# Outputs of two plain f-tiles at a time, a bank each, and weights made in thirds through PSUM

## The chip, the cores and the metric

The kernel runs on one core of a Trainium2 chip. TensorE (PE) multiplies, VectorE (DVE), ScalarE (ACT) and GpSimd (POOL) do elementwise work, and SyncE (SP) issues nearly all DMAs. PE reads its stationary and its moving operand from SBUF and writes to PSUM, which has 8 banks here, one tile of 128x512 floats in each. The metric is the device time of one execution in microseconds: the median of three runs before is 549.28 (547.87 to 549.73). The profiled execution took 550.31, of which 548.5 are the span from the first to the last instruction; 1.8 lie around it.

## The reference

Three stages follow each other. Decayed attention over blocks of 64 positions (2 x 8 heads, 768 positions, width 64):

```python
intra = einsum('bhij,bhjd->bhid', einsum('bhic,bhjc->bhij', qb, kb) * Dmask, vb)
inter = einsum('bhid,bhde->bhie', qb * lam_pow, kv_state)
out[:, :, sl] = intra + inter
kv_state = lam_block * kv_state + einsum('bhsd,bhse->bhde', kb * rev_pow, vb)
```

Its output, as x of 1536 tokens x 512, goes through a gated layer and then a maximum of three:

```python
xn = x / sqrt(mean(x * x) + 1e-6) * rms_g
x = (silu(xn @ w_gate) * (xn @ w_val)) @ w_out      # d_ff 1536: 12 f-tiles of 128
out = max(x @ w1, x @ w2, x @ w3) @ w_out2          # d_ff 768
```

## The kernel before

Every matrix product is made of three (`mm3`): each operand is split into a high part (`wh`, `xh`, `hh`) and the rest (`wl`, `xl`, `hl`), and high by high, high by low and low by high are summed in PSUM. Tokens go in 3 blocks of 512 columns.

**Attention** goes in 12 chunks of 128 tokens. One chunk passes through ten pieces, named by letters: T transposes q and k, C makes scores and state updates, a, b and V mask them and advance the state, M makes the output, U and N norm it, R subtracts to get `xl`, K scales keys. `orders` says in which order the pieces of neighbouring chunks are issued. Chunks 0 to 4 and parts of 5 and 6 run ahead of the gated layer (the loop at L972, here the opening); the rest are issued between the products of blocks 0 and 1, by `gap()`, which is called after every sixth product.

**Weights.** Each tile of weights (a unit: `g` gate, `v` value, `o` output) is loaded as raw 64-bit words (`wraw`, three buffers), made into floats (ACT L238 and L239, DVE L196, L199 and L202, POOL L204), then split: ACT casts `wh` (L167), POOL subtracts to get `wl` (L170). Before, the first stage makes them with `make_unit`, one whole unit at every second `gap()` of block 0, and with `narrow` set the intermediate `mid` lies in SBUF, in W's own place; in the opening it lies in PSUM.

**First stage.** The first four f-tiles are plain: for each block, each f-tile makes `pg` and `pv` (12 products each), gates them, and its 12 output products are added to four accumulators (`acc`) that stay in four banks until the block's four f-tiles are through. Outputs of an f-tile are issued after the next one's `pg` and `pv`. Later f-tiles, and the maxout, use 7 products of half tiles in place of 8; that second stage is not touched but for the very last output tile (`out2`).

Engines take their instructions in the order in which the program issues them, so the order of issue is the order of each queue. The banks are given to tiles as they come free.

Of the kernel before, what the change touches and what calls it, by code (L numbers as in the profile page):

```python
# [18 lines left out]
P = 128  # L19
# [7 lines left out]
def tile_decay_attention_swiglu_maxout(  # L27
# [89 lines left out]

    groups1 = [4]
    PLAIN = sum(groups1)
    unit_list = [(nm, f) for f in range(PLAIN) for nm in "gvo"]  # L120
    for f in range(PLAIN, F1):
        unit_list += [("g", f), ("v", f), ("o", f - 1) if f > PLAIN else None, ("Tg", f), ("Tv", f)]
    unit_list += [("1", 0), ("1", 1), ("o", F1 - 1), ("T1", 0), ("T1", 1), ("2", 0), None, ("2", 1), ("3", 0), ("T2", 0),
# [23 lines left out]
    mid = {}  # L147
    sums_in = {}
    room = [WBUFS, 8]
    pos = {"load": 0, "made": 0, "raw": 0, "step": 0, "gap": 0, "quiet": False, "lag": 3, "narrow": True, "seam": False}  # L150

    def load_to(n):
        while pos["load"] < min(n, len(raw_list)):
# [62 lines left out]
    def begin_unit():  # L216
# [4 lines left out]
        if first_use[key] <= pos["step"] + 6 and at < len(wpools) and (key is None or room[at]):  # L221
# [20 lines left out]
    def make_unit():  # L242

        if stage2:
            finish_unit(*stage2.pop(0))
        if stage1:
            unit = stage1.pop(0)
            for n in range(3):
                words_of_unit(n, *unit)
            stage2.append(unit[:3])  # L250
        begin_unit()

    thirds = []

# [165 lines left out]
    def rest(c):  # L420
# [7 lines left out]
    named = dict(M=(2, mixed), N=(3, normed), C=(1, scores), a=(1, masked(0)), R=(3, rest),  # L428
                 b=(1, masked(1)), U=(2, summed), V=(1, advance), T=(0, lambda c: (loads_to(c + 2), turn(c))),
                 K=(-1, decayed_keys))  # L430
    orders = ["MCaNbTURVK"] * (CPNB + 2) + ["MCaNRbTUVK"] + ["MNCRaUbVTK"] * NCH
    attn_q = [(s_, named[ch][1], s_ - named[ch][0]) for s_ in range(NCH + 3) for ch in orders[s_]
              if (ch == "K") <= s_ - named[ch][0] < NCH]
    gaps = [0, 0]
# [7 lines left out]
    def gap():  # L442


        pos["gap"] += 1
        if not pos["quiet"]:
            if lates:
                third_of_unit()
            elif (pos["gap"] + 5) % (2 if pos["step"] < groups1[0] else 4) == 0:
                make_unit()  # L450
        due.sort(key=lambda e: e[0])
        while due and due[0][0] <= pos["gap"]:
            due.pop(0)[1]()
# [18 lines left out]
    def proj(ps, unit, bh, bl):  # L472
        wh, wl = unit
        for kk in range(KD):
            ks = slice(kk * P, (kk + 1) * P)
            mm3(ps, wh[:, ks], wl[:, ks], bh[:, kk, :], bl[:, kk, :], kk == 0, kk == KD - 1)
            if kk % 2:
                gap()

    def split(dst_h, dst_l, src):  # L480
        nc.scalar.copy(out=dst_h, in_=src)  # L481
# [10 lines left out]
    def drain1(acc, g, j):  # L492
        if g == 0:
            acc_sb[j] = act.tile([P, KD, NB], F32, tag="acc", name="acc_sb", bufs=3)
        for m in range(KD):
            if g == 0:
                nc.scalar.copy(out=acc_sb[j][:, m, :], in_=acc[m])
            else:
                nc.vector.tensor_tensor(out=acc_sb[j][:, m, :], in0=acc[m], in1=acc_sb[j][:, m, :], op=ALU.add)

    def stage_end(j, acc):

# [102 lines left out]
    def hidden1(f, j):  # L605
        bh, bl = x_block(j)
        pg = bank("pg")
        proj(pg, units["g", f], bh, bl)
        pv = bank("pv")
        proj(pv, units["v", f], bh, bl)  # L610
        if j == NBLK - 1:
            free(("g", f), ("v", f))
        sg = act.tile([P, NB], F32, tag="sg", name="sg", bufs=1)
        nc.scalar.activation(out=sg, in_=pg, func=AF.Silu)
        nc.vector.tensor_tensor(out=sg, in0=pv, in1=sg, op=ALU.mult)  # L615
        return sg

    def out1(acc, f, f0, f1, hh, hl):
        wh, wl = units["o", f]
        for m in range(KD):  # L620
            ms_ = slice(m * P, (m + 1) * P)
            mm3(acc[m], wh[:, ms_], wl[:, ms_], hh, hl, f == f0, f == f1)
            if m % 2:
                gap()

    def first_stage():

        acc = []
        before = None
        for now in steps:  # L630
            if now:
                pos["step"] = steps.index(now)
                g, j, f, f0, f1 = now
                if g == 0 and f == f0:
                    while attn_q and attn_q[0][0] <= 6 + 4 * j:
                        attn_step()
                    if j < NBLK - 1:
                        gaps[:] = [(6 * groups1[0], 16)[j], 6 + 4 * (j + 1)]
                if pos["step"] == len(steps) - 1:
                    pos["narrow"] = True  # L640
                r = hidden1(f, j)
                hh = act.tile([P, NB], F32R, tag="hh", name="hh")
                hl = act.tile([P, NB], F32R, tag="hl", name="hl")
                split(hh, hl, r)
                if before:
                    finish()

                def finish(now=now, hh=hh, hl=hl):
                    g, j, f, f0, f1 = now
                    if f == f0:  # L650
                        acc[:] = [bank("acc") for _ in range(4)]
                    out1(acc, f, f0, f1, hh, hl)
                    if f == f1:
                        drain1(acc, g, j)
                    if j == NBLK - 1:
                        free(("o", f))
            before = now
        return finish

# [187 lines left out]
    def out2(g, j, t):  # L847
        last = g == F2 // 2 - 1
        if g == 0 and t == 0:
            acc_sb[j] = act.tile([P, KD, NB], F32, tag="acc", name="acc_sb", bufs=3)  # L850
        ts = slice(t * P, (t + 1) * P)
        acc = bank("acc")
        for d in range(2):
# [4 lines left out]
            nc.tensor.matmul(out=acc, lhsT=hh[:, ts], rhs=wh, start=d == 0, stop=False)  # L858
            nc.tensor.matmul(out=acc, lhsT=hh[:, ts], rhs=wl, start=False, stop=False)  # L859
            nc.tensor.matmul(out=acc, lhsT=hl[:, ts], rhs=wh, start=False, stop=d == 1)  # L860
        y = acc_sb[j][:, t, :]
        if g == 0:
            nc.scalar.copy(out=y, in_=acc)
        else:
            nc.vector.tensor_tensor(out=y, in0=acc, in1=y, op=ALU.add)
        if last:
            r0 = j * NB + t * P
            nc.sync.dma_start(out=out[r0:r0 + P, :], in_=y)
# [75 lines left out]
    with tc.manual_schedule():  # L944
# [27 lines left out]
        for s_ in range(CPNB + 3):  # L972
            if stage1:
                unit_ = stage1.pop(0)
            while attn_q[0][0] == s_:
                fn = attn_q[0][1]
                attn_step()
                if unit_ and fn is named["b"][1]:
                    words_of_unit(0, *unit_)
                elif unit_ and fn is named["U"][1]:  # L980
                    words_of_unit(1, *unit_)
                    if stage2:
                        finish_unit(*stage2.pop(0))
# [6 lines left out]
        pos["narrow"] = True  # L990
        finish = first_stage()
        pos["step"] = len(steps)
        second_stage(finish)
# [31 lines left out]
```

## Time and profile before

| | us |
|---|---|
| median of 3 runs | 549.28 |
| profiled execution | 550.31 |
| its span | 548.5 |
| PE busy | 529.8 (97%) |
| DVE busy | 376.5 (69%) |
| POOL busy | 316.3 (58%) |
| ACT busy | 278.6 (51%) |

A busy PE is pipelined: a product of 512 columns is listed with 0.39 us, but one follows another after 0.23. The shares are means over stages with other limits: the opening ends and the first stage starts at 42.5 us in this execution, attention's last piece on PE is at 128.4. In the profile's rows, "x32" of a 64x64 product stands for 16 products, each in two passes.

### The profile page before, as it was taken

To read this page: it belongs to the slowest core of one execution; us is meant where nothing else is said; L and a number is where in the kernel's file an instruction comes from. 1 tells how busy PE (TensorE), PEld (TensorE's weight loads), DVE (VectorE), ACT (ScalarE), POOL (GpSimd) and SP (SyncE) were. 2 spreads that over 40 slices of the span, in tenths; PEclk is the share of its full clock that TensorE was granted. 3 is DMA by queue.
4 is the path that set the end of the run, shared out by engine and by line. 5 is a ranking of instruction groups with operands and counts; after the bars stand their busy time and mean duration, and the time that the engine had idled before them with its cause. 6 is when DMAs were issued, how large, how long until landed. Compare 5 with 4: busy or idle time off the path is not lost.

```text
span 548.5 us, 9716 instructions
## 1 busy us (share of the span) xinstructions
PE 529.8 (97%) x3722; PEld 438.9 (80%) x3722; DVE 376.5 (69%) x663; ACT 278.6 (51%) x541; POOL 316.3 (58%) x251
## 2 busy tenths in 40 slices
PE   7697979999999999999999999999999999999997
PEld 7685858878888888888888888888888888888885
DVE  6688995447795666657776686877777477684464
ACT  3576754344556665255446426556466755651120
POOL 2469996212899557165455736986387554962050
PEclk9978999999999999999999999999999999999999
DMA  8987566000212222121221312121123222300014
GB/s 193 231 195 185 140 179 155 2 3 0 78 34 82 78 67 86 39 76 39 78 76 39 115 39 77 40 76 38 40 78 114 82 76 75 83 33 0 0 55 176
DMA packets 65454, 44.67 MB, mean 81 GB/s; under 512 B 40064, under 2 KB 61568, under 8 KB 65408
## 3 DMA queue, kind: packets, MB, share of 16 engines
q1 hardware_dynamic: 64704, 44.05, 28.3%
q8 instruction: 29, 0.48, 0.4%
q14 instruction: 17, 0.14, 0.1%
q10 hardware_dynamic: 704, 0.01, 0.1%
HBM read 40.90 MB, written 3.15 MB: 80 GB/s over the span
## 4 chain that ended last, share of the span: by engine, by line
PE 85%; POOL 4%; issue 3%; DVE 3%; SPq 2%; ACT 2%; DMA 1%; POOLq 0%; ACTq 0%
PE p L676 34%; PE r L676 8%; PE acc L468 6%; PE acc L470 6%; PE acc L469 6%; PE q L676 4%; PE acc L859 3%; PE acc L858 3%; PE acc L860 3%; PE pv L468 2%; PE pv L469 2%; PE pv L470 2%; PE pg L468 2%; SPq L92 2%; PE pg L470 2%
## 5 line engine op out<-in xcount | busy, mean ns | idle before, releaser
L170 POOL TENSOR_TENSOR wl<-W,wh 128x512 fp32r<-128x512 f32 x77 | 105.6, 1371 | 39.4 <-ACT wh L167 39.2
L204 POOL TENSOR_TENSOR W<-W,wraw 128x512 int32<-128x512 int32 x60 | 81.3, 1356 | 79.3 <-DVE W L202 70.8
L167 ACT CAST wh<-W 128x512 fp32r<-128x512 f32 x77 | 47.8, 621 | 85.3 <-POOL W L204 84.9
L482 POOL TENSOR_TENSOR hl<-sg,hh 128x512 fp32r<-128x512 f32 x36 | 48.5, 1348 | 25.7 <-ACT hh L481 25.7
L676 PE MATMUL p<-xh,wh 128*128 128x512 f32 x148 | 57.6, 389 | 0.0
L676 PE MATMUL p<-xl,wh 128*128 128x512 f32 x148 | 57.6, 389 | 0.0
L676 PE MATMUL p<-xh,wl 128*128 128x512 f32 x148 | 57.6, 389 | 0.0
L468 PE MATMUL acc<-hh,wh 128*128 128x512 f32 x144 | 56.5, 393 | 0.0
L469 PE MATMUL acc<-hl,wh 128*128 128x512 f32 x144 | 56.1, 389 | 0.0
L470 PE MATMUL acc<-hh,wl 128*128 128x512 f32 x144 | 56.1, 389 | 0.0
L831 DVE TENSOR_TENSOR acc_sb<-acc,acc_sb 128x512 f32<-128x512 f32 x46 | 31.8, 691 | 21.6 <-PE acc L470 20.6
L238 ACT ACTIVATE W<-wraw 128x512 f32<-128x512 f32 x60 | 40.2, 670 | 6.8 <-DMA wraw<-in_moe_w_dram 4.3
L481 ACT CAST hh<-sg 128x512 fp32r<-128x512 f32 x36 | 22.3, 620 | 35.0 <-DVE sg L615 26.4
L239 ACT ACTIVATE wraw<-wraw 128x512 int32<-128x512 uint32 x60 | 39.7, 662 | 0.0
L731 ACT COPY c<-p 128x512 f32<-128x512 f32 x34 | 20.0, 588 | 38.1 <-PE p L676 38.0
L482 POOL TENSOR_TENSOR hl<-m,hh 128x512 fp32r<-128x512 f32 x18 | 24.0, 1343 | 23.0 <-ACT hh L481 22.9
L196 DVE TENSOR_SCALAR mid<-W 128x512 f32<-128x512 f32 x50 | 34.2, 685 | 3.0 <-ACT W L238 3.0
L199 DVE TENSOR_SCALAR mid<-mid 128x512 int32<-128x512 int32 x50 | 34.7, 694 | 0.7
L676 PE MATMUL p<-yh,wh 128*128 128x512 f32 x90 | 35.0, 389 | 0.0
L676 PE MATMUL p<-yl,wh 128*128 128x512 f32 x90 | 35.0, 389 | 0.0
L676 PE MATMUL p<-yh,wl 128*128 128x512 f32 x90 | 35.0, 389 | 0.0
L202 DVE SCALAR_TENSOR_TENSOR W<-wraw,mid 128x512 int32<-128x512 int32 x50 | 34.0, 680 | 1.0
(175 smaller groups left out, 1349.1 us busy)
## 6 DMA issues: line engine op xcount, KB each, us to landing
wraw<-in_moe_w_out_dram SPq DMA_DIRECT2D x18, 512.0 KB, 3.4
wraw<-in_moe_w_dram SPq DMA_DIRECT2D x18, 512.0 KB, 3.6
kn<-in_k_dram SPq DMA_DIRECT2D x12, 256.0 KB, 4.3
qn<-in_q_dram SPq DMA_DIRECT2D x12, 256.0 KB, 5.3
vn<-in_v_dram SPq DMA_DIRECT2D x12, 256.0 KB, 4.2
wraw<-in_moe_w_gate_dram SPq DMA_DIRECT2D x12, 256.0 KB, 3.0
wraw<-in_moe_w_gate_dram SPq DMA_DIRECT2D x24, 128.0 KB, 3.6
wraw<-in_moe_w_val_dram SPq DMA_DIRECT2D x12, 256.0 KB, 3.0
```

Source lines behind the costliest of these rows:

```text
L167: nc.scalar.copy(out=wh, in_=W.bitcast(F32))
L170: nc.gpsimd.tensor_tensor(out=wl, in0=W.bitcast(F32), in1=wh.bitcast(F32), op=ALU.subtract)
L196: nc.vector.tensor_scalar(out=mid[key].bitcast(F32), in0=W.bitcast(F32), scalar1=LEAST, scalar2=MOST, op0=ALU.max, op1=ALU.min)
L199: nc.vector.tensor_scalar(out=mid[key], in0=mid[key], scalar1=0x07FFFFFF, scalar2=3, op0=ALU.bitwise_and, op1=ALU.logical_shift_left)
L204: nc.gpsimd.tensor_tensor(out=W, in0=W, in1=lo, op=ALU.add)
L238: nc.scalar.activation(out=W.bitcast(F32), in_=hi.bitcast(F32), func=AF.Abs)
L239: nc.scalar.activation(out=lo, in_=lo.bitcast(U32), func=AF.Copy, scale=2.0 ** -29)
L468: nc.tensor.matmul(out=out, lhsT=wh, rhs=xh_, start=first, stop=False)
L469: nc.tensor.matmul(out=out, lhsT=wh, rhs=xl_, start=False, stop=False)
L470: nc.tensor.matmul(out=out, lhsT=wl, rhs=xh_, start=False, stop=last)
L482: nc.gpsimd.tensor_tensor(out=dst_l, in0=src, in1=dst_h.bitcast(F32), op=ALU.subtract)
L676: nc.tensor.matmul(out=ps, lhsT=w[:, ks], rhs=r[:, o + k, :], start=first and k == 0 and n == 0, stop=k == 1 and n == 2, skip_group_check= ...
```

## The change

Blocks 0 and 1 hold two f-tiles' `hh` and `hl` and then make their outputs together (`out_two`): for each of four output slices one bank takes both f-tiles' six products, and is then copied to SBUF (first pair, ACT) or added to it (second pair, DVE). This is issued between the next f-tile's `pg` and `pv`. Block 2 stays as it was. The list of units follows: two `g` and `v`, then two `o`, and one `g` ahead of the `o`. `spread()` is called after every third product; it issues attention's pieces, and a third of a unit in three calls of four. `narrow` stays off until the last step, so that `mid` lies in PSUM. In the opening, weights are loaded and begun one chunk later. In step 0 the products with `xl` come last. The last output tile of the kernel is made and stored in two halves of 256 columns. Not shown here: the lines of `hidden1` that only move code into it.

```diff
-    unit_list = [(nm, f) for f in range(PLAIN) for nm in "gvo"]
+    unit_list = []
+    for f in range(0, PLAIN, 2):
+        unit_list += [("g", f), ("v", f), ("g", f + 1), ("v", f + 1), ("o", f), ("o", f + 1)]
+        if f:
+            unit_list.insert(6 * f // 2 - 2, unit_list.pop(6 * f // 2))
...
-    orders = ["MCaNbTURVK"] * (CPNB + 2) + ["MCaNRbTUVK"] + ["MNCRaUbVTK"] * NCH
+    orders = ["MCaNbTURVK"] * (CPNB + 2) + ["MCNRabTUVK"] + ["MNCRaUbVTK"] * NCH
...
             if lates:
                 third_of_unit()
-            elif (pos["gap"] + 5) % (2 if pos["step"] < groups1[0] else 4) == 0:
-                make_unit()
         due.sort(key=lambda e: e[0])
         while due and due[0][0] <= pos["gap"]:
             due.pop(0)[1]()
+        spread()
+
+    def spread():
+        pos["half"] += 1
+        if not lates and pos["half"] % 4:
+            third_of_unit()
         if gaps[0]:
...
+        todo = [(kk, w, x) for kk in range(KD) for w, x in ((wh, bh), (wh, bl), (wl, bh))]
+        if early:
+            todo.sort(key=lambda e: e[2] is bl)
+        for n, (kk, w, x) in enumerate(todo):
+            nc.tensor.matmul(out=ps, lhsT=w[:, kk * P:(kk + 1) * P], rhs=x[:, kk, :], start=n == 0,
+                             stop=n == len(todo) - 1)
+            if n % 6 == 5:
                 gap()
+            elif n % 6 == 2:
+                spread()
...
+    def out_two(j, two):
+        if two[0][0] == 0:
+            acc_sb[j] = act.tile([P, KD, NB], F32, tag="acc", name="acc_sb", bufs=3)
+        for m in range(KD):
+            ms_ = slice(m * P, (m + 1) * P)
+            ps = bank("acc")
+            for d, (f, hh, hl) in enumerate(two):
+                wh, wl = units["o", f]
+                mm3(ps, wh[:, ms_], wl[:, ms_], hh, hl, d == 0, d == 1)
+                (spread, gap)[d]()
+            y = acc_sb[j][:, m, :]
+            if two[0][0] == 0:
+                nc.scalar.copy(out=y, in_=ps)
+            else:
+                nc.vector.tensor_tensor(out=y, in0=ps, in1=y, op=ALU.add)
...
+                    gaps[:] = [(36, 34)[j], 6 + 4 * (j + 1)]
+            if pos["step"] == len(steps) - 1:
+                pos["narrow"] = True
+            two.append(hidden1(f, j, waiting.pop() if waiting else None))
+            if j < NBLK - 1:
+                if len(two) == 2:
+                    waiting.append(lambda j=j, two=two: out_two(j, two))
+                    two = []
+                continue
...
+        ends = last and (j, t) == (NBLK - 1, NB // P - 1)
+        for cs in (slice(0, HF), slice(HF, NB)) if ends else (slice(0, NB),):
+            if cs.start:
+                acc = bank("acc")
+            for n, (x, w) in enumerate(todo):
+                nc.tensor.matmul(out=acc[:, cs], lhsT=x[:, ts], rhs=w[:, cs], start=n == 0, stop=n == len(todo) - 1)
...
-            load_to(pos["load"] + 1)
-            if s_ > 1:
+            if s_:
+                load_to(pos["load"] + 1)
+            if s_ > 2:
                 begin_unit()
-        pos["narrow"] = True
```

Three places where the order of issue moves. First, PE at the start of the first stage, from the last piece of the opening on; before:

```order
L400 MATMUL pm<-ones,sq 128x1 x4
L468 MATMUL pg<-xh,wh 128x512
L469 MATMUL pg<-xl,wh 128x512
L470 MATMUL pg<-xh,wl 128x512
L468 MATMUL pg<-xh,wh 128x512
L469 MATMUL pg<-xl,wh 128x512
L470 MATMUL pg<-xh,wl 128x512
```

and now:

```order
L393 MATMUL pm<-ones,sq 128x1 x4
L475 MATMUL pg<-xh,wh 128x512
L475 MATMUL pg<-xh,wl 128x512
L475 MATMUL pg<-xh,wh 128x512
L367 MATMUL px_909<-qs,S 64x64
L367 MATMUL px_910<-qs,S 64x64
```

The product with `xl` was second and is now ninth at the earliest, and piece M of the next chunk (`px`), whose end piece N (`pb`, which needs `ri`) follows at once, begins after three products and no longer after six.

Second, POOL from chunk 3's `xl` (the last that block 0 needs) and `ri` of chunk 4 on; before:

```order
L426 TENSOR_TENSOR xl<-x,xh 128x4x128
L404 TENSOR_TENSOR ri<-ms,mhalf 128x1
L170 TENSOR_TENSOR wl<-W,wh 128x512
L204 TENSOR_TENSOR W<-W,wraw 128x512
L284 TENSOR_TENSOR kd<-kn,Tm 128x512
L170 TENSOR_TENSOR wl<-W,wh 128x512
L204 TENSOR_TENSOR W<-W,wraw 128x512
L426 TENSOR_TENSOR xl<-x,xh 128x4x128
```

and now:

```order
L419 TENSOR_TENSOR xl<-x,xh 128x4x128
L397 TENSOR_TENSOR ri<-ms,mhalf 128x1
L174 TENSOR_TENSOR wl<-W,wh 128x512
L208 TENSOR_TENSOR W<-W,wraw 128x512
L277 TENSOR_TENSOR kd<-kn,Tm 128x512
L174 TENSOR_TENSOR wl<-W,wh 128x512
L419 TENSOR_TENSOR xl<-x,xh 128x4x128
L208 TENSOR_TENSOR W<-W,wraw 128x512
```

The kinds stand almost as they did, but the first `wl` shown was the fourth unit's and is now the second's (`v` of f-tile 0): the opening prepared fewer units.

Third, PE at the first output products, with the tiles' numbers (`acc_` is the bank's tile, `hh_1120` f-tile 0's and `hh_1269` f-tile 1's); before:

```order
L468 MATMUL acc_1252<-hh_1066,wh_899 128x512
L469 MATMUL acc_1252<-hl_1067,wh_899 128x512
L470 MATMUL acc_1252<-hh_1066,wl_900 128x512
L468 MATMUL acc_1253<-hh_1066,wh_899 128x512
L469 MATMUL acc_1253<-hl_1067,wh_899 128x512
L470 MATMUL acc_1253<-hh_1066,wl_900 128x512
```

and now:

```order
L465 MATMUL acc_1385<-hh_1120,wh_1225 128x512
L466 MATMUL acc_1385<-hl_1121,wh_1225 128x512
L467 MATMUL acc_1385<-hh_1120,wl_1226 128x512
L465 MATMUL acc_1385<-hh_1269,wh_1332 128x512
L466 MATMUL acc_1385<-hl_1270,wh_1332 128x512
L467 MATMUL acc_1385<-hh_1269,wl_1333 128x512
```

The fourth product went to a second bank of the same f-tile and now goes to the same bank, with the next f-tile's `hh` and the second `o` unit.

## Rows read from the trace of the kernel before

**Rows 1.** The page: busy times, and the granted TensorE clock in 40 slices

```profile
PE 529.8 (97%) x3722; PEld 438.9 (80%) x3722; DVE 376.5 (69%) x663; ACT 278.6 (51%) x541; POOL 316.3 (58%) x251
...
PEclk9978999999999999999999999999999999999999
```

**Rows 2.** Busy time by stretch: PE, PEld, DVE, ACT, POOL, clock, DMA share, GB/s

```profile
42.00:62.00 20.00, 17.51 (x256) 13.38 (x260) 17.58 (x29) 14.00 (x32) 19.37 (x17) 0.91 0.60 159
62.00:82.00 20.00, 15.93 (x242) 12.55 (x231) 19.11 (x40) 12.20 (x25) 18.55 (x14) 1.00 0.73 186
...
122.00:162.00 40.00, 40.00 (x203) 33.16 (x195) 31.88 (x43) 21.50 (x43) 26.18 (x18) 1.00 0.09 27
```

**Rows 3.** PE's waits: line, what it waited for, us in total, times, longest

```profile
PE sc L323 <- issue: 3.9, 2, 2.6
PE sc L318 <- ACT x L387: 2.3, 2, 2.1
PE pg L469 <- POOL xl L426: 1.7, 1, 1.7
...
PE pg L468 <- ACT xh L417: 1.0, 1, 1.0
PE px L374 <- DVE S L348: 0.9, 1, 0.9
PE pm L400 <- ACT sg L614: 0.7, 1, 0.7
```

**Rows 4.** PE in order of time, opening: start, us, instruction [idle before]

```profile
18.60 0.34 PE L323 MATMUL sc<-vn,kd 64*64 64x64 f32 x8 [1.24 <-issue]
...
25.92 0.69 PE L323 MATMUL sc<-vn,kd 64*64 64x64 f32 x29 [2.62 <-issue]
```

**Rows 5.** PE in order of time, start of the first stage

```profile
42.52 0.50 PE L468 MATMUL pg<-xh,wh 128*128 128x512 f32 x1 [1.01 <-ACT xh L417]
44.76 0.79 PE L469 MATMUL pg<-xl,wh 128*128 128x512 f32 x1 [1.74 <-POOL xl L426]
...
48.90 0.49 PE L413 MATMUL pb<-ident,ri 128*128 128x128 f32 x2
```

**Rows 6.** The chain that ended last: start, us, what

```profile
97.17 0.44 PE pk L294 x4
...
108.45 0.44 PE pk L294 x4
...
173.65 5.44 PE p L676 x24
...
544.97 0.69 DVE acc_sb L865
```

**Rows 7.** POOL in order of time, 42 to 65 us

```profile
42.42 1.07 POOL L284 TENSOR_TENSOR kd<-kn,Tm 128x512 f32<-128x512 f32 x1
43.43 1.27 POOL L426 TENSOR_TENSOR xl<-x,xh 128x512 fp32r<-128x512 f32 x1
44.66 0.56 POOL L404 TENSOR_TENSOR ri<-ms,mhalf 128x1 f32<-128x1 f32 x1
45.17 1.28 POOL L170 TENSOR_TENSOR wl<-W,wh 128x512 fp32r<-128x512 f32 x1
46.41 1.47 POOL L204 TENSOR_TENSOR W<-W,wraw 128x512 int32<-128x512 int32 x1
...
63.77 1.79 POOL L170 TENSOR_TENSOR wl<-W,wh 128x512 fp32r<-128x512 f32 x1 [0.84 <-ACT wh L167]
```

**Rows 8.** DVE by line and shape, 42 to 100 us: busy, mean ns

```profile
L202 DVE SCALAR_TENSOR_TENSOR W<-wraw,W 128x512 int32<-128x512 int32 x8 | 11.1, 1387 | 0.3
...
L202 DVE SCALAR_TENSOR_TENSOR W<-wraw,mid 128x512 int32<-128x512 int32 x1 | 0.7, 689 | 0.1
```

**Rows 9.** DMA issues by tile: engine, count, KB each, us to landing

```profile
wraw<-in_moe_w_gate_dram SPq DMA_DIRECT2D x12, 256.0 KB, 3.0
...
out_dram<-acc_sb SPq DMA_DIRECT2D x12, 256.0 KB, 2.0
```

More of the change, by code (lines that the diff above doesn't have):

```diff
@@ L149, in tile_decay_attention_swiglu_maxout @@
     room = [WBUFS, 8]
-    pos = {"load": 0, "made": 0, "raw": 0, "step": 0, "gap": 0, "quiet": False, "lag": 3, "narrow": True, "seam": False}
+    pos = {"load": 0, "made": 0, "raw": 0, "step": 0, "gap": 0, "half": 0, "quiet": False, "lag": 3, "narrow": True, "seam": False}
     def load_to(n):
@@ L240, in begin_unit @@
             stage1.append((key, W, at, lo, hi))
[L242 to L251, printed above, removed]
     thirds = []
@@ L470, in mm3, with proj @@
         nc.tensor.matmul(out=out, lhsT=wl, rhs=xh_, start=False, stop=last)
-    def proj(ps, unit, bh, bl):
+    def proj(ps, unit, bh, bl, early=False, then=None):
         wh, wl = unit
[L474 to L477, printed above, removed]
+        todo = [(kk, w, x) for kk in range(KD) for w, x in ((wh, bh), (wh, bl), (wl, bh))]
[5 more added lines that the diff above has]
+            if n % 6 == 5:
                 gap()
+            elif n % 6 == 2:
+                spread()
+                if n == 2 and then:
+                    then()
     def split(dst_h, dst_l, src):
@@ L490, in lower, with drain1 @@
         eng.tensor_tensor(out=dst_l, in0=src, in1=dst_h.bitcast(F32), op=ALU.subtract)
-    def drain1(acc, g, j):
-        if g == 0:
-            acc_sb[j] = act.tile([P, KD, NB], F32, tag="acc", name="acc_sb", bufs=3)
+    def drain1(acc, j):
+        acc_sb[j] = act.tile([P, KD, NB], F32, tag="acc", name="acc_sb", bufs=3)
         for m in range(KD):
[L496 to L499, printed above, removed]
+            nc.scalar.copy(out=acc_sb[j][:, m, :], in_=acc[m])
     def stage_end(j, acc):
@@ L603, in sums_of_quarters, with hidden1 @@
         pos["quiet"] = True
-    def hidden1(f, j):
+    def hidden1(f, j, between=None):
         bh, bl = x_block(j)
         pg = bank("pg")
-        proj(pg, units["g", f], bh, bl)
+        proj(pg, units["g", f], bh, bl, early=pos["step"] == 0)
+        if between:
+            between()
+        sg = act.tile([P, NB], F32, tag="sg", name="sg", bufs=1)
         pv = bank("pv")
-        proj(pv, units["v", f], bh, bl)
+        proj(pv, units["v", f], bh, bl, then=lambda: nc.scalar.activation(out=sg, in_=pg, func=AF.Silu))
         if j == NBLK - 1:
             free(("g", f), ("v", f))
-        sg = act.tile([P, NB], F32, tag="sg", name="sg", bufs=1)
-        nc.scalar.activation(out=sg, in_=pg, func=AF.Silu)
         nc.vector.tensor_tensor(out=sg, in0=pv, in1=sg, op=ALU.mult)
-        return sg
+        hh = act.tile([P, NB], F32R, tag="hh", name="hh")
+        hl = act.tile([P, NB], F32R, tag="hl", name="hl")
+        split(hh, hl, sg)
+        return f, hh, hl
     def out1(acc, f, f0, f1, hh, hl):
@@ L622, in out1 @@
             mm3(acc[m], wh[:, ms_], wl[:, ms_], hh, hl, f == f0, f == f1)
-            if m % 2:
-                gap()
+            (spread, gap)[m % 2]()
+    def out_two(j, two):
+        if two[0][0] == 0:
+            acc_sb[j] = act.tile([P, KD, NB], F32, tag="acc", name="acc_sb", bufs=3)
+        for m in range(KD):
[10 more added lines that the diff above has]
+                nc.vector.tensor_tensor(out=y, in0=ps, in1=y, op=ALU.add)
     def first_stage():
@@ L629, in first_stage, with finish @@
         before = None
+        two, waiting = [], []
         for now in steps:
-            if now:
-                pos["step"] = steps.index(now)
-                g, j, f, f0, f1 = now
[L634 to L639, printed above, removed]
-                    pos["narrow"] = True
[L641 to L656, printed above, removed]
+            g, j, f, f0, f1 = now
+            pos["step"] = steps.index(now)
+            if f == f0:
+                while attn_q and attn_q[0][0] <= 6 + 4 * j:
+                    attn_step()
+                if j < NBLK - 1:
[3 more added lines that the diff above has]
+            two.append(hidden1(f, j, waiting.pop() if waiting else None))
+            if j < NBLK - 1:
+                if len(two) == 2:
+                    waiting.append(lambda j=j, two=two: out_two(j, two))
+                    two = []
+                continue
+            if before:
+                finish()
+            def finish(now=now, hh=two[0][1], hl=two[0][2]):
+                g, j, f, f0, f1 = now
+                if f == f0:
+                    acc[:] = [bank("acc") for _ in range(4)]
+                out1(acc, f, f0, f1, hh, hl)
+                if f == f1:
+                    drain1(acc, j)
+                free(("o", f))
+            two = []
             before = now
@@ L852, in out2 @@
         acc = bank("acc")
+        todo = []
         for d in range(2):
@@ L857, in out2 @@
             hh, hl = parts[j, d]
-            nc.tensor.matmul(out=acc, lhsT=hh[:, ts], rhs=wh, start=d == 0, stop=False)
-            nc.tensor.matmul(out=acc, lhsT=hh[:, ts], rhs=wl, start=False, stop=False)
-            nc.tensor.matmul(out=acc, lhsT=hl[:, ts], rhs=wh, start=False, stop=d == 1)
+            todo.extend(((hh, wh), (hh, wl), (hl, wh)))
         y = acc_sb[j][:, t, :]
[L862 to L868, printed above, removed]
+        r0 = j * NB + t * P
+        ends = last and (j, t) == (NBLK - 1, NB // P - 1)
[4 more added lines that the diff above has]
+                nc.tensor.matmul(out=acc[:, cs], lhsT=x[:, ts], rhs=w[:, cs], start=n == 0, stop=n == len(todo) - 1)
+            if g == 0:
+                nc.scalar.copy(out=y, in_=acc)
+            else:
+                nc.vector.tensor_tensor(out=y[:, cs], in0=acc[:, cs], in1=y[:, cs], op=ALU.add)
+            if last:
+                nc.sync.dma_start(out=out[r0:r0 + P, cs], in_=y[:, cs])
         if (j, t) == (NBLK - 1, NB // P - 1):
@@ L986, in tile_decay_attention_swiglu_maxout @@
                     stage2.append(unit_[:3])
-            load_to(pos["load"] + 1)
-            if s_ > 1:
+            if s_:
+                load_to(pos["load"] + 1)
+            if s_ > 2:
                 begin_unit()
-        pos["narrow"] = True
         finish = first_stage()
```

## The prediction

> **What bounds the kernel now.** I read the page's busy times first, then the table by stretch, then PE's waits, and last the order of time around the longest of them. PE is busy for 97% of the span and its clock is lowest in two early slices, 27.4 to 54.8 us [rows 1]. The table by stretch says where the rest lies: from 122 us on PE has no idle time and runs at full clock, and between 42 and 82 it is busy for 33.4 of 40 us [rows 2]. There DVE is busy for 36.7 and POOL for 37.9 of 40, so in that stretch PE is fed by two engines that are full. The list of waits gives the amounts [rows 3]: 2.3 us of scores waiting for ACT's x (these two share no data: it is a PSUM bank that x still reads), 0.9 for DVE's S, 0.7 for a bank of ACT's sg, together 3.9; at the start of the stage 1.0 for `xh` and 1.7 for `xl`; and in the opening 3.9 that no semaphore explains. So what the change can win lies before 122 us, and in the last 4 us, where the chain leaves PE for the last add and store [rows 6]. The products themselves, some 430 us from 122 on, are neither fewer nor faster: a full product costs 5.44/24 = 0.227 us [rows 6] before and after.
>
> **Start of the first stage.** Before, PE is done with the opening's last piece at 41.5 (42.52 less its wait of 1.01), waits for `xh`, makes one product, waits 1.74 for `xl`, and after six products and piece M it begins `pb` at 48.90 [rows 5]. Now N stands ahead of the first mask for that chunk, which brings DVE's multiply for `xh` forward by one mask and four state steps; `xh` should be there by 41.5. The next seven products need no `xl`, and `xl` is there at 44.7 [rows 7]. What is late next is `ri`: piece M follows after three products and N right behind it, so PE reaches `pb` at 41.5 + 3 x 0.227 + 1.5 = 43.7 (M taken as a third of a chunk's 4.5 us, below), but POOL makes this `ri` behind `xl`, from 44.66 to 45.2 [rows 7]. PE waits 1.5 there and begins `pb` at 45.2, three products short of where it was at 48.90. These cost 0.7, so the gain is 48.9 - 45.2 - 0.7 = 3.0. Bounds: 1.5, if `ri` comes later or the clock falls as in this execution (0.91 in the stretch from 42 to 62 [rows 2]), and 4.4, if `ri` comes with the rest of an earlier opening.
>
> **Block 0: weights through PSUM, and banks.** The last step of a unit on DVE takes 1387 ns with its intermediate in SBUF and 689 in PSUM [rows 8]: eight units save 8 x 0.70 = 5.6 us of DVE. POOL gains too: its `wl` takes 1.28 behind a unit made through PSUM (45.17) and up to 1.79 behind one made in SBUF (63.77) [rows 7]; eight of these can give back 4 us. The adds of the second pair cost DVE 4 x 0.69 (like the add at the end [rows 6]) for each of blocks 0 and 1, 2.8 us, issued when the weights are done, and the copies of the first pair take the place of four copies at the block's end. The output's bank is held for six products and not for a block: of 8 banks, four came away for good from the second step on, now one at a time, and one is used for `mid`. So the 3.9 us of waits for banks and S should go for the most part.
>
> What is late next is POOL, since the opening leaves it one unit more to make. From `xl` at 43.43 to the `wl` of the second `o` it has 22 instructions: 3 `xl` at 1.23, 3 `ri` at 0.51, 6 `wl` at 1.24, 5 W and 2 `hl` at 1.25, 3 `kd` at 1.01 (distances between starts in [rows 7], W and `hl` taken like `wl`), 24.5 us, so 67.9 if it never idles. PE needs that `wl` for the sixth product of the first `out_two`. It has 65 products before it (14.8 us), and two chunks of attention less one transposition and one sum, and M, N and C of a third. A chunk costs PE 108.45 - 97.17 = 11.28 less the 30 products between, 4.5 us [rows 6]; 2 x 4.5 + 3.5 = 12.5. 41.5 + 1.5 + 14.8 + 12.5 = 70.3. POOL so has 2.4 us for waits of its own, of which the stretch before shows one of 0.84 [rows 7]; three of these would use it up. I put the new waits of block 0 at 1.5 us, between 0 and 5.4 (as much as the old 3.9 and the 1.5 on top), and the gain at 3.9 - 1.5 = 2.4.
>
> **The opening.** One weight tile fewer is queued ahead of the loads of chunks 2 to 6, and ACT and DVE have one unit less. PE's two waits of 1.24 and 2.62 us have no releaser, and lie inside a group of 32 passes over the same `vn` and `kd`, with 8 and 29 of the 32 still to come [rows 4]: the operands were there, so it was the instructions that were late, on queues full of data. The clock is lowest in the slice after the second (27.4 to 41.1 us) [rows 1]. The weights now come behind chunk 3's q and k and no longer ahead of them, but the queues stay as full at first, so I expect the first wait to stay and the second to shrink, and take 1.5 us. Bounds: 0, and 4, all of 3.9.
>
> The Trainium skill says, in "Runtime: NRT & Kernel Launch", section Instruction fetch mechanics, that the sequencer streams straight-line code by itself and that crossing a block of it is mostly hidden. By that rule the 3.9 us [rows 4] would be late data, which a load taken out of the way would bring in time, and the sum would be 2.4 us lower than mine; the split inside one group of operands speaks against it.
>
> **The end.** Twelve half products follow each other after at least 0.11 us (four 128-column products with a load of weights each take 0.44 [rows 6]) and at most as long as full ones, 0.227; I take 0.12, near the first, so 1.44 against 6 x 0.227 = 1.36. The add of half a tile saves half of 0.69 less its fixed part, 0.27, and the store of 128 KB is at most 0.5 faster than the 2.0 us of 256 KB [rows 9]. Together -0.3, between -0.8 and +1.3.
>
> Free of cost are: the earlier Silu (ACT has 6 of 20 us free in the stretch [rows 2]); finer pieces of attention in block 1, where DVE has nothing of the weights to make; the unit order, which puts each unit ahead of its first use as before. If that cover went, it would show as a wait for `wl`.
>
> **Sum.** 3.0 + 2.4 + 1.5 + 0.3 = 7.2. The profiled execution's 550.31 becomes 543.1; it ran 1.03 above the median, so 542.1 for the median of new runs.
>
> **Rivals.** (a) *Everything goes*: POOL, relieved by DVE, is never late, the instruction waits go with the queue, and the clock stays up. 4.0 + 3.5 + 4.0 + 0.5 = 12, or 537. For it: all of these waits are of full engines and queues that the change relieves. Against: POOL starts a unit behind.
>
> (b) *The work is only shifted*: the opening gains nothing and POOL's queue holds PE in block 0 about as long as the banks did. 3.0 less 1.5 of new waits, 1 to 2 us, or 547.5. For it: POOL at 97% and 93% [rows 2] is the fullest engine there and loses no instruction. Against: its 4 us from shorter `wl`.
>
> (c) *Slower: the raw tiles*. A load of unit k may start when POOL's W of unit k-3 is done. Before, ACT began unit k two rounds behind that; now it begins in the first third of the next round but one, one round and a third later, and a load takes 3.0 us to land [rows 9]. A round is four calls, each of three products and about one of a chunk's ten pieces, 4 x (0.68 + 0.45) = 4.5 us. If ACT stands still for the load, it holds back kT, qT, x and `wh` behind it. PE needs the `wl` of the second `v` of the second pair, eight units after the one that ends at 46.4 [rows 7], for its 111th product, at 41.5 + 1.5 + 25 + 18 = 86 (110 products and four chunks): so this decides from 5.0 us per unit on. POOL alone needs 4.0 (31.7 us for the 28 instructions up to there, with the distances above). With load 3.0, ACT's two passes and DVE's three at 0.69 each [rows 8] one after the other, 6.5 us, that unit would come at 98, 12 late, and the kernel would take 542.1 + 12 = 554. Against it: three buffers let three units overlap.
>
> (d) *Nothing happens* because PE's waits are only renamed: 549.
>
> **How the numbers follow.** Forecast (539 to 546.5): 0.55. (a): 0.15. (b): 0.17, half of it (0.08) faster by more than 0.3%. (c): 0.09. (d): 0.04. 0.3%, 1.65 us, is about what a measurement of this kernel can tell from no change. Faster: 0.55 + 0.15 + 0.08 = 0.78. Within 0.3%: 0.09 + 0.04 = 0.13. Slower: 0.09. The range leaves out (c), (d) and the faster half of (a): 537.5 to 548.5; the forecast's own is 539 to 546.5.
>
> **What would show it.** In the profile after: PE's waits on `xl` and on x gone; a wait of 1 to 2 us of `pb` for `ri` at the start; DVE's last step of a unit at about 690 ns and POOL's `wl` at about 1300; any new wait of PE a POOL `wl` or `hl` at the first `out_two`; in the opening one wait without releaser left. From the end of attention on, the two kernels should run in parallel. I am wrong if ACT waits for `wraw` in the first stage and PE behind it, or if the stretch after 122 us shows idle PE.

## The result, and the profile after

The changed kernel takes 555.15 us (median of four runs, 553.57 to 556.28) against 548.74 of the kernel before in the same series: ratio 1.0114, 95% interval 1.0081 to 1.0147. It is slower, by some 6 us, where 542.1 was forecast. The profiled execution took 553.57 us, its span 551.8. It lies 1.6 us below the median, and the profiled one of before (550.31) 1.6 above, so the two profiles show 3.3 of the 6.4 us between the medians.

The page of the changed kernel, busy times and granted clock:

```profile
PE 532.0 (96%) x3728; PEld 439.0 (80%) x3728; DVE 375.2 (68%) x672; ACT 279.7 (51%) x541; POOL 309.8 (56%) x251
...
PEclk9997989999899999999999999999999999999999
```

The first low slice of [rows 1] is gone, the second is lower, and two others have come. The table by stretch, columns as in [rows 2]:

```profile
42.00:62.00 20.00, 17.31 (x212) 13.74 (x203) 14.08 (x31) 12.68 (x29) 13.18 (x12) 0.83 0.57 148
62.00:82.00 20.00, 17.53 (x253) 13.50 (x252) 13.09 (x32) 14.07 (x31) 15.36 (x15) 0.91 0.55 146
...
122.00:162.00 40.00, 37.43 (x157) 30.17 (x157) 35.58 (x47) 20.26 (x37) 25.18 (x17) 0.96 0.12 35
```

DVE fell from 17.6 and 19.1 us of 20 to 14.1 and 13.1, POOL from 19.4 and 18.6 to 13.2 and 15.4: these two are no longer full, and neither is PE. After 122 us, where PE never paused before, 2.6 us are missing. PE's waits (line, what it waited for, total, times, longest) and the same waits in order of time:

```profile
PE pb L406 <- POOL ri L397: 3.0, 3, 1.5
PE pm L393 <- DVE ss L384: 2.6, 1, 2.6
PE acc L466 <- POOL hl L486: 2.6, 2, 2.3
PE acc L465 <- ACT wh L171: 1.6, 1, 1.6
...
PE acc L467 <- POOL wl L174: 0.6, 1, 0.6
```

```profile
17.45 0.34 PE L316 MATMUL sc<-vn,kd 64*64 64x64 f32 x8 [0.46 <-issue]
...
27.60 0.50 PE L311 MATMUL sc<-qT,kT 64*64 64x64 f32 x18 [0.86 <-issue]
...
40.34 0.49 PE L406 MATMUL pb<-ident,ri 128*128 128x128 f32 x2 [1.49 <-POOL ri L397]
46.09 0.59 PE L393 MATMUL pm<-ones,ss 128*128 128x1 f32 x2 [2.58 <-DVE ss L384]
71.64 0.51 PE L465 MATMUL acc<-hh,wh 128*128 128x512 f32 x1 [1.62 <-ACT wh L171]
73.00 0.80 PE L467 MATMUL acc<-hh,wl 128*128 128x512 f32 x1 [0.63 <-POOL wl L174]
...
143.67 0.50 PE L466 MATMUL acc<-hl,wh 128*128 128x512 f32 x1 [2.29 <-POOL hl L486]
```

In the first stage none of the waits of [rows 3] for x, S, sg, xh or xl is left. Three new ones (at 46, 72 and 143 us) each end in a stretch at a lower granted clock:

```profile
46.00:56.00 10.00, 9.80 (x78) 7.78 (x78) 7.21 (x17) 6.03 (x15) 7.42 (x7) 0.68 0.59 153
70.00:80.00 10.00, 7.75 (x61) 5.97 (x60) 7.71 (x20) 7.53 (x17) 6.86 (x6) 0.83 0.59 147
140.00:150.00 10.00, 7.71 (x28) 5.88 (x27) 8.73 (x11) 5.32 (x10) 7.32 (x6) 0.83 0.17 54
```

The two levels are 1.2 and 2.4 GHz, so a mean of 0.68 over 10 us is 6.4 us at the lower one, and each 0.83 is 3.4. Half of such time is lost: 3.2, 1.7 and 1.7 us. The profiled execution of before had its own low stretches, in the opening and at the start of the stage:

```profile
26.00:34.00 8.00, 7.89 (x176) 7.50 (x176) 5.58 (x17) 4.94 (x12) 4.62 (x6) 0.58 0.85 205
36.00:48.00 12.00, 8.62 (x169) 6.70 (x168) 10.32 (x23) 7.84 (x19) 10.09 (x11) 0.86 0.89 212
```

A ledger of the two profiled spans, 548.5 to 551.8:

| part | before | after | difference |
|---|---|---|---|
| first product of the first stage begins | 42.52 | 36.46 | -6.1 |
| idle time of PE from there to the second stage | 5.7 | 10.2 | +4.5 |
| lost to the lower clock in the same part | 1.7 | 6.8 | +5.1 |
| second stage, first product to last | 371.4 | 371.5 | +0.1 |
| end of the last product to the end | 3.57 | 3.14 | -0.4 |

(Before: 1.74 + 0.94 + 2.14 + 0.19 + 0.70; after: 1.49 + 2.58 + 1.62 + 0.63 + 1.28 + 0.28 + 2.29; the clock from 0.86 and, with 0.90 over 36 to 48 and over 48 to 70 us and twice 0.83, 1.2 + 2.2 + 1.7 + 1.7.) The sum is 3.2 of the 3.3 seen. So in these two executions the first stage begins 6.1 us sooner, and all of that is spent between 40 and 145 us.

**Where it goes first.** ACT in order of time in the changed kernel:

```profile
38.66 0.68 ACT L243 ACTIVATE wraw<-wraw 128x512 int32<-128x512 uint32 x1
43.23 0.66 ACT L242 ACTIVATE W<-wraw 128x512 f32<-128x512 f32 x1 [3.89 <-DMA wraw<-in_moe_w_gate_dram]
43.79 0.64 ACT L243 ACTIVATE wraw<-wraw 128x512 int32<-128x512 uint32 x1
44.33 0.65 ACT L378 ACTIVATE sq<-px 128x256 f32<-128x256 f32 x2
44.86 1.15 ACT L380 ACTIVATE x<-px,g_sb 128x128 f32<-128x128 f32 x4
```

ACT asks at 39.3 for the raw tile of the third gate, which no product needs before the second pair. Its load was issued at 37.55 and lands at 43.2:

```profile
35.48 0.96 SPq L92 DMA_DIRECT2D qn<-in_q_dram  x1
37.55 1.68 SPq L161 DMA_DIRECT2D wraw<-in_moe_w_gate_dram  x3
```

`sq` stands behind it on ACT's queue, `ss` behind `sq` on DVE, and PE reaches `pm` and waits for `ss`:

```profile
39.36 0.69 DVE L200 TENSOR_SCALAR mid<-W 128x512 f32<-128x512 f32 x1
45.01 1.02 DVE L384 TENSOR_REDUCE ss<-sq 128x128 f32<-128x512 f32 x1 [4.97 <-ACT sq L378]
```

**And last.** At 143 us PE waits for block 1's last `hl`, which POOL made late, in this order:

```profile
136.80 1.74 POOL L494 TENSOR_TENSOR zl<-sums,zh 128x512 fp32r<-128x512 f32 x1
138.49 1.76 POOL L208 TENSOR_TENSOR W<-W,wraw 128x512 int32<-128x512 int32 x1
140.22 1.72 POOL L494 TENSOR_TENSOR zl<-sums,zh 128x512 fp32r<-128x512 f32 x1
141.91 1.71 POOL L486 TENSOR_TENSOR hl<-sg,hh 128x512 fp32r<-128x512 f32 x1
```

Its `hh` was ready at 140.3 (139.72 and 0.62):

```profile
139.72 0.62 ACT L485 CAST hh<-sg 128x512 fp32r<-128x512 f32 x1 [3.95 <-DVE sg L616]
```

`out_two` of this pair stands between the gate and the value product of block 2's first tile, so that 12 products lie between the pair's last value product and its first output; in the kernel before it was 24.

### The profile page after: what moved, and what is told of

The parts are those of the page before. It is cut to its first block, busy times and chain, and to the rows that moved or that the text cites. A ratio compares the mean times of both kernels' runs of the same rounds, so it can differ in the third digit from the quotient of the medians.

```text
span 551.8 us, 9731 instructions
## 1 busy us (share of the span) xinstructions
PE 532.0 (96%) x3728; PEld 439.0 (80%) x3728; DVE 375.2 (68%) x672; ACT 279.7 (51%) x541; POOL 309.8 (56%) x251
## 4 chain that ended last, share of the span: by engine, by line
PE 85%; POOL 5%; DVE 3%; issue 3%; ACT 1%; DMA 1%; SPq 0%; POOLq 0%; ACTq 0%; DVEq 0%
PE p L697 34%; PE acc L888 9%; PE r L697 8%; PE acc L467 6%; PE acc L466 6%; PE acc L465 6%; PE pv L475 5%; PE q L697 4%; PE pg L475 3%; PE px L367 2%; POOL W L208 1%; POOL wl L174 1%; POOL hl L486 1%; DMA wraw<-in_moe_w_gate_dram 1%; POOL zl L494 1%
## 5 line engine op out<-in xcount | busy, mean ns | idle before, releaser
L174 POOL TENSOR_TENSOR wl<-W,wh 128x512 fp32r<-128x512 f32 x77 | 101.8, 1323 | 55.3 <-ACT wh L171 52.7
L466 PE MATMUL acc<-hl,wh 128*128 128x512 f32 x144 | 57.4, 399 | 2.6 <-POOL hl L486 2.6
L465 PE MATMUL acc<-hh,wh 128*128 128x512 f32 x144 | 58.0, 403 | 1.6 <-ACT wh L171 1.6
L467 PE MATMUL acc<-hh,wl 128*128 128x512 f32 x144 | 57.5, 400 | 0.6 <-POOL wl L174 0.6
L200 DVE TENSOR_SCALAR mid<-W 128x512 f32<-128x512 f32 x57 | 39.0, 684 | 3.4 <-ACT W L242 3.4
L203 DVE TENSOR_SCALAR mid<-mid 128x512 int32<-128x512 int32 x57 | 39.5, 693 | 0.8
L206 DVE SCALAR_TENSOR_TENSOR W<-wraw,mid 128x512 int32<-128x512 int32 x57 | 38.8, 681 | 1.6
```

## The experiments

Each time stands beside the kernel before in the same series (547.3 to 547.7 us), with the ratio to it; the changed kernel's is 1.0114, from the series of the result: it was not run again beside its variants.

**ACT's passes in the last third of a round** (begin_last). Lines of `third_of_unit`:

```diff
-            thirds.extend([lambda: (begin_unit(), words_of_unit(0, *unit)),
+            thirds.extend([lambda: words_of_unit(0, *unit),
...
-                           lambda: (later[0] and later[0](), words_of_unit(2, *unit), stage2.append(unit[:3]))])
+                           lambda: (later[0] and later[0](), words_of_unit(2, *unit), stage2.append(unit[:3]),
+                                    begin_unit())])
```

> The changed kernel with one edit: of the three thirds of a round of weights, ACT's two passes over the raw tile stand in the last and no longer in the first. Theory A (raw tiles): ACT reaches the raw tile of the third gate before its load has landed, waits 3.9 us, and holds back sq and x behind it; PE then waits 2.6 us for ss and runs 6.8 us at 1.2 GHz, which costs 3.4 more. Two thirds of a round (some 3 us) later the load is there or nearly so: the wait for ss and most of the slow stretch go, 555 becomes 548 to 551. Rival B (POOL's queue): POOL is the engine that is late, and with the passes later each unit only comes later: the waits turn into waits for ri, wl and wh, and the time is 554 to 558.

Measured: 546.08, ratio 0.9962 (0.9943 to 0.9982). 1.5% less than the changed kernel, some 8 us, more than Theory A asked. ACT in this kernel:

```profile
39.27 0.67 ACT L243 ACTIVATE wraw<-wraw 128x512 int32<-128x512 uint32 x1
39.83 0.63 ACT L379 ACTIVATE sq<-px 128x256 f32<-128x256 f32 x2
...
44.33 0.68 ACT L242 ACTIVATE W<-wraw 128x512 f32<-128x512 f32 x1 [0.28 <-DMA wraw<-in_moe_w_gate_dram]
```

The load lands 1 us later still (44.3), but ACT asks for it 4.7 us later, and `sq` is ahead of it. PE does not wait for `ss`; the waits at the first `out_two` shrink from 1.62 and 0.63 to 0.60 and 0.63, and the clock stays at 1.00 through both places. Theory B falls.

**The piece of attention ahead of the third**, in the same call (pieces_first):

```diff
     def spread():
-        if not lates and pos["half"] % 4:
-            third_of_unit()
+        weights = not lates and pos["half"] % 4
...
+        if weights:
+            third_of_unit()
```

> The changed kernel with one edit: where a call makes both a third of a weight unit and a piece of attention, the piece is issued first. The load of the third gate stays as late as it was. Theory A says that the harm is in what stands behind ACT's wait: ACT waits for the raw tile again, 2 to 4 us, but sq and x of that call are ahead of it, PE's wait of 2.6 us for ss goes and with it the slow stretch: 549 to 551. Rival E: xh, kT, qT and sg still stand behind the wait, so that PE only waits one piece later, on xh, sc or ri, as long as before: 553 to 556.

Measured: 550.32, ratio 1.0048 (1.0031 to 1.0065), 0.7% less. The wait for `ss` went. ACT:

```profile
40.40 1.14 ACT L380 ACTIVATE x<-px,g_sb 128x128 f32<-128x128 f32 x4
42.28 0.62 ACT L410 CAST xh<-x 128x512 fp32r<-128x512 f32 x1 [0.74 <-DVE x L408]
43.16 0.67 ACT L242 ACTIVATE W<-wraw 128x512 f32<-128x512 f32 x1 [0.27 <-DMA wraw<-in_moe_w_gate_dram]
```

The load comes no sooner. With `sq`, x and `xh` done in the meantime, its wait is 0.27; I had expected 2 to 4, with the damage gone. At the first `out_two` PE still waits 2.12 for `wh` (0.60 in begin_last), with the clock at 0.83 over 66 to 76 us behind it, and it waits 0.99 behind ACT's `sg`; so this edit gains less than half of what begin_last does.

**A fourth raw tile** (raw4), so that the third gate's load need not wait for POOL:

```diff
+            spare = pos["load"] in (4, 8)
-            t = wp.tile([P, KD, 2 * P], I32, tag="raw", name="wraw", bufs=3)
+            t = (att if spare else wp).tile([P, KD, 2 * P], I32, tag="raw", name="wraw", bufs=1 if spare else 3)
```

(and `kd` and `x` with two buffers for three, for its room)

> The changed kernel with a fourth raw tile for the fifth and the ninth load (room for it from one kd and one x tile less), so that the third gate's load, the fifth, need not wait until POOL has done with the second unit. Theory A: the load is late because it waits for its tile; now it lands before ACT asks, ACT's wait of 3.9 us goes, PE's wait for ss with it: 548 to 551. Rival F (the queues): what makes the load late is the traffic of q, k and v, 5.7 us from issue to landing where 3 is usual; issued earlier it pushes these back, and PE waits for them as long: 553 to 556.

Measured: 548.99, ratio 1.0023 (1.0005 to 1.0042). The time is Theory A's, the mechanism only in part:

```profile
35.70 0.89 SPq L92 DMA_DIRECT2D qn<-in_q_dram  x1
36.64 2.08 SPq L162 DMA_DIRECT2D wraw<-in_moe_w_gate_dram  x3
```

```profile
42.31 0.68 ACT L243 ACTIVATE W<-wraw 128x512 f32<-128x512 f32 x1 [1.77 <-DMA wraw<-in_moe_w_gate_dram]
```

With a tile free, the load still stands behind `qn` in SP's queue, goes out 0.9 us sooner, and again takes 5.7 us to land. So the tile's reuse was a small part of the delay; its place in the queue and the traffic are the rest, as Rival F had it. Part of the smaller wait is that this kernel's PE comes later: it waits 1.75 for x (`pq` at 36.9), of which there is one buffer less. With that wait comes a slow stretch of its own (0.66 over 36 to 46 us), so this time is no clean measure of the load.

**The opening's loads and first passes as before** (open_before):

```diff
-            if s_:
-                load_to(pos["load"] + 1)
-            if s_ > 2:
+            load_to(pos["load"] + 1)
+            if s_ > 1:
                 begin_unit()
```

> The changed kernel with the opening's loads and first passes as in the kernel before (a load in each of seven steps, a unit begun from the third step on). Theory A: the opening loses what it had gained, 5 to 6 us, and the raw tile of the third gate is no longer late in the first stage, which gives 4 to 6 us back: 553 to 557. Rival D (the thirds are what costs, wherever the loads stand): the opening's gain is lost and nothing comes back: 560 to 562.

Measured: 551.50, ratio 1.0061 (1.0038 to 1.0084), a little below Theory A's range: Rival D falls. The opening ends at 38.91 for 36.46, and the wait for `ss` is 0.98 for 2.58. ACT does not wait for the load there, but 2.25 us for a W tile, until a `wl` of POOL is done; that this comes of one unit more under way is not shown.

**Only the new opening, in the kernel before** (before_opening: the same lines in reverse, and chunk 6's order):

> The kernel before with only the new opening (a load from the second step on, a unit begun from the fourth, and the order of chunk 6's pieces). Theory A: the later load holds up ACT in the first stage whoever makes the weights, so most of the 6 us gained by the opening is lost behind ACT's wait: 546 to 549. Rival D (the thirds are what costs): the gain of the opening stays whole: 542 to 544.

Measured: 547.62, ratio 1.0002 (0.9985 to 1.0019). The number is Theory A's, but not the mechanism: ACT waits for no raw tile here. PE waits 2.85 us for `xl` and 2.51 for `wl` of POOL, with one unit fewer made in the opening. And its profiled execution, the lowest of its twelve (546.37), begins the stage at 36.6, 5.9 us sooner than the profiled one of before: the medians do not show that much.

**Block 1's second output pair behind both products** (out_later):

```diff
-        if between:
+        if between and j < NBLK - 1:
             between()
...
         nc.vector.tensor_tensor(out=sg, in0=pv, in1=sg, op=ALU.mult)
+        if between and j == NBLK - 1:
+            between()
```

> The changed kernel with one edit: block 1's second pair of output tiles comes after both products of block 2's first hidden tile, and no longer between them. Theory A: the wait of 2.3 us for hl at 143 us is there because only the gate's 12 products stand between this hl and its use; 24 products give it 2.7 us more, the wait goes, and with it the 3.4 us at 1.2 GHz behind it (1.7 us): 555 becomes 551. Rival C: hl is late because POOL and DVE make the sums of x at that time; those are not moved, so something else of the same queue is late next, and the time stays at 554 to 556.

Measured: 548.95, ratio 1.0025 (1.0008 to 1.0043), 0.9% less, some 5 us. The wait at 143 us is gone and the stretch is full (PE busy, clock 1.00):

```profile
136.00:146.00 10.00, 10.00 (x46) 8.28 (x45) 9.12 (x10) 3.72 (x7) 9.96 (x7) 1.00 0.15 54
```

POOL makes this `hl` at 141.69 as before, but PE asks for it at 143.7. Rival C falls. Not all of the 5 us is this edit's: up to here both kernels are the same, yet in this profile the clock stays at 1.00 over 46 to 56 us (the last section), where the changed kernel's 0.68 cost 3.2.

**Both edits**, begin_last's and out_later's.

> The changed kernel with both edits: ACT's passes in the last third of a round, and block 1's second output pair behind both products. If the two waits are independent, the gains add: begin_last's 546 less the wait of 2.3 and its slow stretch of 1.7, 541 to 543. Rival: the second edit lets another unit slip or moves the sums of x, and the kernel stays at 545 to 547.

Measured: 542.45, ratio 0.9908 (0.9891 to 0.9924). As forecast, though the 1.5% and 0.9% measured singly come to 2.1% together. This kernel is faster than the one before, at about the time forecast for the change, which does not yet bear out the forecast's terms. The median of the granted clocks is 0.990 in the runs of the kernel before in this series, 1.000 here and 0.987 in the changed kernel. The span times what is missing to 1, as an estimate of what the lower clock costs where PE sets the time, makes 5.5, 0.0 and 7.2 us; without it the three take 542.0, 542.1 and 547.7. By this estimate the gain of 5 us is that of a clock that no longer falls, and all else that the change and the edits save and cost nearly cancels out.

**Both edits, and two pieces of attention moved** (piece R behind U in chunk 6's row, an empty piece ahead of the last N):

> Both edits, and two moves of attention pieces: in chunk 6's row the lower half of x (piece R) behind the sum U, so that POOL makes ri ahead of xl at the start of the first stage, and an empty piece ahead of the last N, so that three more products lie between the last ri and its pb. If PE's waits of 1.5 and 1.25 us for ri stand on the path, 2 to 2.7 us less than with both edits alone, 538.5 to 541. Rival: xl, or what follows it on POOL, is late in ri's place, and the time is that of both edits within 1 us.

Measured: 542.95, ratio 0.9927 (0.9900 to 0.9954): nothing. The first `pb` begins at 39.29 for 40.64, yet the 97th product of the stage starts at 78.82 for 78.98: the waits at the first `out_two` (0.61 and 0.63) remain, and what was gained ahead of them is given back by then. The wait of 1.25 later became 0.56, and the next for `hl` rose from 0.26 to 0.93.

**Both edits, intermediate words in SBUF** (`pos["narrow"] = True` ahead of `first_stage`):

> Both edits, but the intermediate words of a unit in SBUF in the first stage too, as in the kernel before, and not in PSUM. DVE's last step of a unit then takes 1.39 us for 0.69 and POOL's lower parts 1.3 to 1.8. If these two engines still feed PE in block 0, as my prediction had it, 3 to 6 us slower than both edits alone. Rival: they have slack by now, and nothing changes (within 1 us).

Measured: 545.35, ratio 0.9969 (0.9953 to 0.9985), 0.6% or 3 us slower, at the lower edge of what was expected. DVE's last step between 42 and 100 us, in this kernel and with both edits alone:

```profile
L206 DVE SCALAR_TENSOR_TENSOR W<-wraw,W 128x512 int32<-128x512 int32 x9 | 10.5, 1165 | 0.2
```

```profile
L206 DVE SCALAR_TENSOR_TENSOR W<-wraw,mid 128x512 int32<-128x512 int32 x9 | 6.2, 687 | 0.5
```

That these steps make the 3 us is not shown. PE waits 1.30 us for `wh` at the first `out_two` (0.61 with both edits alone) and 1.22 for `hl` at 95 us (none), but 0.27 for the first `ri` (1.49). A slow stretch from 37.5 to 41 us, ahead of these waits, costs 1.7, and the median clock of the runs is 0.996 for 1.000, by the same estimate 2 of the 3 us.

**Both edits, outputs of one f-tile at a time** in blocks 0 and 1:

```diff
-            if j < NBLK - 1:
+            if j < 0:
                 if len(two) == 2:
```

> Both edits, but outputs in blocks 0 and 1 are of one f-tile at a time, as in the kernel before, with four banks held for a whole block. My prediction gave the waits for banks 3.9 us, less 1.5 of new waits: 545 to 547 by that. Rival: with weights in thirds a bank comes free in time, and PE's waits for the o weights come one tile at a time, so that nothing is lost: 541 to 543.5.

Measured: 551.04, ratio 1.0072 (1.0044 to 1.0100), 1.6% or 9 us slower, beyond both. In block 0 it loses 3.3 us (97th product at 83.02 for 78.98, with a start 0.7 later). In block 1 it meets a wait I had not thought of, 3.65 us for `ri`, which POOL makes behind an `hl` that waits for its `hh`, and a slow stretch follows (0.84 over 122 to 132 us):

```profile
119.69 1.26 POOL L487 TENSOR_TENSOR hl<-sg,hh 128x512 fp32r<-128x512 f32 x1 [8.05 <-ACT hh L486]
120.91 0.55 POOL L398 TENSOR_TENSOR ri<-ms,mhalf 128x1 f32<-128x1 f32 x1
```

```profile
121.52 0.66 PE L407 MATMUL pb<-ident,ri 128*128 128x128 f32 x2 [3.65 <-POOL ri L398]
```

So two tiles at a time is worth its place in this kernel; how much of the 9 us is banks alone stays open.

**Both edits, the thirds of a unit in one call of four:**

```diff
-        if not lates and pos["half"] % 4:
-            third_of_unit()
+        if not lates and pos["half"] % 4 == 2:
+            for _ in range(3):
+                third_of_unit()
```

> Both edits, but the three thirds of a unit are issued in one call of every four and no longer one in each of three. If spreading them is what lets pieces of attention through on ACT and DVE, the units hold these up for 3 to 4 us each and PE waits for kT, x or S: 545 to 549. Rival: the queues of ACT and DVE have room enough, and it makes no difference within 1 us: 541.5 to 543.5.

Measured: 541.88, ratio 0.9896 (0.9869 to 0.9924), the fastest of all, though not told apart from both edits alone. With both edits in, the thirds as such bring nothing.

**Both edits, and the fourth raw tile:**

> Both edits, and the fourth raw tile. With ACT's passes in the last third the loads have slack enough by theory A, and the tile adds nothing: 541.5 to 543.5. Rival: the raw tile still paces the units of block 0, whose last ones PE waits for (0.6 us for wh and for wl at 65 us); then 539 to 541.

Measured: 543.95, ratio 0.9938 (0.9919 to 0.9957), 0.4 us above the range of Theory A. It gains nothing, and pays the wait of 1.75 us for x in the opening that its tile's room costs.

## Why the prediction was wrong

- *Start of the first stage, 3.0.* What it named happened: no waits for `xh` and `xl`, and `pb` waits 1.49 us for `ri` (forecast 1.5). It stopped one piece too soon: `ss`, next in line, was 2.58 late, and with the slow stretch behind it the 25th product starts at 55.26, where it was 54.91 before, with one T, one M and one N of attention more behind it (some 2 us of PE). So of the 6.1 us by which the stage began sooner some 2 are left there.
- *Block 0, 2.4.* The old waits went, and DVE's step and POOL's lower parts are as short as priced (684 ns between 42 and 100 us; 1293 for `wl`). The new wait stands at the first `out_two`, where it was put: 2.25 us, within its bounds, with 1.7 of slow clock that had no price. Its cause was wrong: not a full POOL, which had 6.8 of 20 us idle from 42 to 62, but, for 1.08 of the 2.25, ACT, which at 68 us waits once more for a raw tile, with the `wh` that PE waits for behind it (begin_last, without that wait, keeps 1.23):

```profile
68.29 0.67 ACT L242 ACTIVATE W<-wraw 128x512 f32<-128x512 f32 x1 [1.08 <-DMA wraw<-in_moe_w_gate_dram]
```

- *The opening, 1.5.* 6.1 in the profiled executions, beyond the bound of 4.0. The waits without a releaser, which the prediction put down to late instructions, fell from 3.86 to 1.32; the rest is above all the slow stretch from 26 to 34 us (0.58), which I had read and not priced. How much is typical is uncertain: with the same opening code, the profiled execution of out_later again had one of 1.70 us and began the stage at 39.4; and in before_opening, the kernel before with this opening, the median did not fall, though there waits of 2.85 and 2.51 us stand against it. The Trainium skill ("Runtime: NRT & Kernel Launch", Instruction fetch mechanics) calls the crossing of an instruction block mostly hidden; no run here shows where a block ends, and each profile has at least one wait without a releaser in the first 36 us, of 0.2 to 2.6 us (0.2 in all in raw4).
- *The end, 0.3.* Measured 0.4; the half products follow each other after 0.12 us, as taken.
- *The step that failed* is rival (c) at 0.09, and the 3.0 us for a load's landing in it: in the sum, ACT's wait for a raw tile stands at nothing. Measured, ACT stood 3.89 us, PE waited 2.58 behind it, and the slow stretch cost 3.2 more; with ACT's passes two thirds of a round later (begin_last) the ratio fell from 1.0114 to 0.9962. The mechanism of (c), ACT standing still for a raw tile with other work behind it, is the one that decided, and its 554 stands near the 555 measured; its place and price were wrong, so that agreement is partly luck. I followed the tile's reuse through a steady round, and found the trouble at the eighth unit, at 86 us, if each unit took 5 us. It needed no steady state: in the first call of the stage the load, which the new opening issues behind q of the next chunk, took 5.7 us on the full queues of that stretch (a DMA share of 0.91 over 36 to 46 us; 3.0 is the median of the whole span [rows 9]). My reason against it, that three buffers let three units overlap, says nothing on one load that is late.
- *Terms missing*: the wait for `hl` at 143 us, 2.29 with 1.7 of slow clock behind it. Moving `out_two` between two products halves the distance between an operand's making and its use. I checked that for the weights and not for `hl`, at the seam to block 2 where POOL also makes the sums of x. I had named idle PE after 122 us as a sign of being wrong, beside ACT's wait for `wraw`, but given it no term. The lower clock, too, stood in one bound of the start and in no term, neither for what it cost the kernel before nor for what new waits might bring.

## What to carry to other kernels

Before an operation that needs a load is put at the head of a round, look what stands behind it on that engine's in-order queue, and read the load's landing time from its own stretch, not from a median over the span: the same load cost ACT 0.28 us and PE nothing when two calls of other work stood ahead of it. When a consumer is moved nearer to its producer, recount the distance for each of its operands, at the busiest place and not only in the middle of a block. And an idle gap of PE may have a second price behind it, so a wait forecast wants a bound with the slow stretch added.

## What had not been expected of the hardware

The lower clock came behind some waits and not behind others of the same size: after 2.58 us (`ss`, changed kernel) the granted clock fell to a mean of 0.68 over 46 to 56 us; in out_later, after 2.31 us at the same place, it stayed at 1.00:

```profile
46.00:56.00 10.00, 7.58 (x81) 5.32 (x79) 7.18 (x16) 7.96 (x21) 5.88 (x6) 1.00 0.69 177
```

With both edits and the words in SBUF (both_narrow) it fell to half from 37.5 to 41 us with no PE wait above 0.27 us in the 14 us before. What PE did before differs too little in these traces to say why.
